# The way back of a Fourier filter, from sums and differences of conjugate pairs in sixteen 32x32 tiles

## The chip, the cores and the metric

The kernel runs on one core of a Trainium2 chip. The metric is the device time of one execution in microseconds; before the change it is 2642.59 us (median of 5 runs, 2641.39 to 2644.59).

## The reference

```python
# x (8, 3008, 256), filt_r and filt_i (1505, 256), w_in (256, 2048), w_out (2048, 256), all fp32
X = np.fft.rfft(x, axis=1)
Y = X * (filt_r + 1j * filt_i)[None]
y = np.fft.irfft(Y, n=3008, axis=1)
h = y.reshape(24064, 256) @ w_in
g = np.where(h > 0, h, np.exp(np.minimum(h, 0)) - 1)
out = g @ w_out
```

Every sequence is filtered along its 3008 positions in the frequency domain, and an ELU layer of two matrix products follows.

## The kernel before, in words

The transform of length 3008 = 47 x 64 is done as matrix products in two steps. Step one (x_unit, a_unit) works on the 64-point part. Step two (b_unit) is the 47-point part: for four frequencies k2 at a time (a group g of eight) it makes real and imaginary parts in PSUM (tiles psr and psi), and multiplies them on DVE with the filter f into four products: sr, si, p and q. On POOL p is added to sr and q to si. The way back starts with bi_unit, 47 points again, from these sums into PSUM (tiles pva and pvb), and ACT copies the result into the tile t3. y_write puts it into DRAM (yd), y_read gets it back in another order, and n_unit does the 64 points of the way back. Between step one and step two the data also goes through DRAM (z_write, z_read).

The ELU layer is done with Strassen-like products of seven terms instead of eight: up_steps makes seven products with w_in (L421, tiles phs, pha, phd), forms sums on DVE (L429, "add b22" and its like), and applies the ELU with ACT (L438, L439) and DVE (L443); down_steps makes the seven products with w_out (L503, PSUM tiles po) and sums them at the last of four (L519, in part deferred as c_unit). o_unit transposes on DVE and writes the output.

All runs in an order written out by hand. A batch has 24 quads; a quad is one pass of the outermost loop, with seven U steps (s1, s2, s6, s5, s7, s3, s4: two matmuls each of 128x128 by 256 columns, or 224 for m = 0) and seven D steps, in the order "UUDUDDU", place 0, "DUUDUDD", place 1. In quads of the set `opens` the order is "DUUDUDDU", place 0, "DUUDUD", place 1. The units of the filter are put into place 0 or place 1 of a quad by a dictionary. So the filter of batch b runs between the matrix products of batch b - 1. Batch 0 is filtered ahead of the loop, in a part of its own (0 to 96 us).

Four PSUM banks (psM, tags m0 to m3) go round between the U steps and the units: `banks` is a list in order of release, a unit takes its first ones and puts them back when they are read.

b_unit and bi_unit do not use the PE array as one 128x128 array. Their inputs lie in partitions 0 to 47 (LO) and 64 to 111 (HI), and their outputs in partitions 0 to 63 and 64 to 127, so that four matmuls work in four separate 64x64 tiles of the array; the rows of a tile are given by the partitions of the input, its columns by the partitions of the output. Per batch there are eight b_units, in quads 9 to 16 of the batch (place 1), and eight bi_units, two quads behind.

The special tables for group 0 (index 1 of gb, gr and gi) hold the frequencies k2 = 0 and 32, which pair with themselves.

Timing of the units in a batch (quads from the batch's start t; a number above 23 lies in the next batch): x_unit 1, 1, 4, 4, 7, 7, each pair with an a_unit in the same quad; f_read and z_read of group g in 7 + g; b_unit in 9 + g; bi_unit and y_write of group g in 11 + g; n_unit in 20, 25, 29, 32, 36, 40; c_unit of half m in 24 + 4 m + 5, o_unit one later. Seen from the following batch, c_unit so stands in quads 5, 9, 13, 17, 21 and 1, and o_unit in 6, 10, 14, 18, 22 and 2.

f_read is issued from POOL's queue; x_load, z_write, z_read, y_write, y_read and the output writes from SP's.

Of the kernel before, what the change touches and what calls it, by code (L numbers as in the profile page):

```python
# [11 lines left out]
FP32 = mybir.dt.float32  # L12
U32 = mybir.dt.uint32
AXT = mybir.ActivationFunctionType
ALU = mybir.AluOpType
# [11 lines left out]
P = 128  # L27
D = 256
# [3 lines left out]
K2 = 32  # L32
XC = 4
NXC = H // XC
NG = K2 // 4
# [6 lines left out]
def _make_tables():  # L42
# [51 lines left out]
    gr[0:24, 1, 0:24], gr[24:48, 1, 24:48] = m0 * c0.T, m3 * c3.T  # L94
    gi[0:24, 1, 24:48], gi[24:48, 1, 0:24] = -m0 * s0.T, -m3 * s3.T
    lie = np.concatenate([2 * np.arange(24), 2 * np.arange(24) + 1])
    gb[:, :, lie] = gb[:, :, :48].copy()
# [6 lines left out]
    once = np.stack([np.eye(P), gf.reshape(P, P)], 1)  # L104
    return [t.astype(np.float32) for t in (ta, tn, np.stack([gb, gr, gi], 1), tf, once)]

# [7 lines left out]
def kernel(  # L114
# [10 lines left out]

    ta_d, tn_d, gs_d, tf_d, once_d = [
        nc.inline_tensor(t, name=n + "_t").ap()
        for t, n in zip(_make_tables(), ("ta", "tn", "gs", "tf", "once"))
    ]

    def pool(name, bufs, **kw):
        return ctx.enter_context(tc.tile_pool(name=name, bufs=bufs, **kw))
# [7 lines left out]
    t2p = pool("t2p", 2)  # L140
    sp = pool("sp", 2)
    qp = pool("qp", 1)
    t3p = pool("t3p", 2)
    t4p = pool("t4p", 2)
# [6 lines left out]

    gs = glob.tile([P, 3, 2, 64], FP32, name="gs")
    gb, gr, gi = (gs[:, i] for i in range(3))

# [3 lines left out]
    edges = glob.tile([P, 2], FP32, name="edges")  # L158
    fd = fdp.tile([NG, 2, 48, 2, 2, D], FP32, name="fd")

    xs, tas, tns, t1s, t2s, ss, t3s, t4s, zs, yds, ys, g_of, po_of, cs_, sds = ({} for _ in range(15))
# [8 lines left out]
    def bank(name, shape=(P, 2, D)):  # L170
        i = banks.pop(0)
        return i, psM.tile(list(shape), FP32, tag="m%d" % i, name=name)
# [120 lines left out]

    def f_read(b, g, t=None):
        t = fbufs[(b * NG + g) % FBUFS] if t is None else t
        for a, r in enumerate((LO, HI)):
            nc.gpsimd.dma_start(t[r].rearrange("p c u d -> p (c u d)"), fd[g, a].rearrange("q c u d -> q (c u d)"))

    def tile_mm(ps, table, k, rhs, special):
# [3 lines left out]

    def b_unit(b, g, f=None, gb=gb, pq=None, between=None):
        t = t2s.pop((b, g))
        f = fbufs[(b * NG + g) % FBUFS] if f is None else f
        (i0, re), (i1, im) = (bank(n) for n in ("psr", "psi"))
        for o, a in ((0, 0), (64, 2)):
            for ps, k in ((re, LO), (im, HI)):
                tile_mm(ps[o:o + 64], gb, k, [t[:, a:a + 2, :]], g == 0 and a == 0)  # L310
        if between:
            between()
        sr, si = (sp.tile([P, 2, D], FP32, tag=n, name=n) for n in ("sr", "si"))
        p, q = pq or (qp.tile([P, 2, D], FP32, tag=n, name=n) for n in ("sp", "sq"))

        nc.vector.tensor_tensor(out=sr, in0=re, in1=f[:, 0], op=ALU.mult)
        nc.vector.tensor_tensor(out=si, in0=re, in1=f[:, 1], op=ALU.mult)
        nc.vector.scalar_tensor_tensor(out=p, in0=im, scalar=-1.0, in1=f[:, 1], op0=ALU.mult, op1=ALU.mult)  # L318
        nc.vector.tensor_tensor(out=q, in0=im, in1=f[:, 0], op=ALU.mult)
        banks.extend((i0, i1))  # L320
        if b == 0:

            ss[b, g] = [sr, p], [si, q]
            return
        nc.gpsimd.tensor_tensor(out=sr, in0=sr, in1=p, op=ALU.add)  # L325
        nc.gpsimd.tensor_tensor(out=si, in0=si, in1=q, op=ALU.add)
        ss[b, g] = [sr], [si]

    def bi_unit(b, g):
        s = ss.pop((b, g))  # L330
        t = t3s[b, g] = t3p.tile([P, 4, D], FP32, tag="t3", name="t3")
        if b == 0:

            pa, pb = (psO.tile([P, 2, 256], FP32, tag="po%d" % i, name="po%d" % i)
                      for i in ((0, 1) if g > 2 and g % 2 else (2, 3)))
        else:
            (i0, pa), (i1, pb) = (bank(n) for n in ("pva", "pvb"))
        for o, table, sv in ((0, gr, s[0]), (64, gi, s[1])):
            for ps, k in ((pa, LO), (pb, HI)):
                tile_mm(ps[o:o + 64], table, k, sv, g == 0 and k == LO)  # L340
        nc.scalar.activation(out=t[:, 0:2, :], in_=pa, func=AXT.Copy)  # L341
        nc.scalar.activation(out=t[:, 2:4, :], in_=pb, func=AXT.Copy)
        if b > 0:
            banks.extend((i0, i1))

    def y_write(b, g, queues=(nc.sync, nc.sync)):
        if g == 0:
            yds[b] = yd.tile([K2, 96, D], FP32, tag="yd", name="yd")
        t = t3s.pop((b, g))
        for a, r in enumerate((LO, HI)):  # L350
            queues[a].dma_start(yds[b][4 * g:4 * g + 4, 48 * a:48 * a + 48, :].rearrange("u r d -> r u d"), t[r])

# [285 lines left out]
    def f_arrange():  # L638

        for c, src in enumerate((filt_r, filt_i)):  # L640
# [14 lines left out]
            nc.gpsimd.dma_start(fd[0, 0, 47:48, c, 1, :], raw(src, 4, [[D, 1], [1, D]]))  # L655

    with tc.manual_schedule():


        with tc.tile_pool(name="boot", bufs=1) as bp:  # L660
            ff = bp.tile([P, NG, 2, 2, D], FP32, name="ff")
            once = bp.tile([P, 2, P], FP32, name="once")
            eye, gf = once[:, 0], once[:, 1].rearrange("p (v q) -> p v q", v=2)
            pq = [bp.tile([P, 2, D], FP32, name="pq%d" % i) for i in range(2)]
            zt[0] += [bp.tile([P, 16 * ROWS], FP32, name="zt%d" % i) for i in range(2)]
# [50 lines left out]
            for g in range(NG):  # L716
                f_read(0, g, ff[:, g])
                if 3 <= g < 5:
                    w_fetch(g + 7)
# [6 lines left out]
            for g in range(NG + 2):  # L726
                back = (lambda g=g: bi_unit(0, g - 2)) if g >= 2 else None
                if g < NG:
                    b_unit(0, g, ff[:, g], gf, pq if g % 2 else None, back)
                else:  # L730
                    back()
                if g < 4:
                    t_first(g + 4)
                if g < 5:
                    w_float(g + 7)
                if g < 3:
                    w_join(g + 7)
                    w_split(g + 8)
                if g == 2:
                    w_split(11)  # L740
                if g >= 2:
                    y_write(0, g - 2, (nc.sync, nc.scalar if g == NG + 1 else nc.sync))
                if g == 7:
                    w_join(10)
                    w_join(11)
                    w_split(12)
                    w_split(13)
# [19 lines left out]
        PER = 24  # L767

        plan, opens = {}, set()

        def at(quad, place, fn, *a):
            plan.setdefault((quad, place), []).append((fn, a))
# [5 lines left out]
        for c in range(2, XBUFS):  # L778
            at(c - 2, 0, x_load, 1, c)
        for i, f in enumerate(fbufs):  # L780
            at(3 + i, 1, nc.vector.memset, f, 0.0)
        for b in range(B):
            t = (b - 1) * PER
            if b > 0:
                for c, s in enumerate((1, 1, 4, 4, 7, 7)):
                    at(t + s, 0, x_unit, b, c)
                    if c % 2 == 0:
                        opens.add(t + s + 1)
                        at(t + s, 1, a_unit, b, c)
                    nb, nxt = (b, c + XBUFS) if c + XBUFS < NXC else (b + 1, c + XBUFS - NXC)  # L790
                    if nb < B:
                        at(t + s, 1, x_load, nb, nxt)
                    at(t + s, 1, z_write, b, c)
                for g in range(NG + 2):
                    s = t + 9 + g
                    if g >= 2:
                        at(s, 1, bi_unit, b, g - 2)
                    if g < NG:
                        at(s, 1, b_unit, b, g)
                    if g >= 2:  # L800
                        at(s, 1, y_write, b, g - 2)
                for g in range(NG):
                    s = t + 7 + g
                    at(s, 1, f_read, b, g)
                    at(s, 1, z_read, b, g)
            for m, (s, place) in enumerate(((20, 0), (25, 1), (29, 1), (32, 0), (36, 0), (40, 0))):
                if b > 0 or m > 0:
                    at(t + s - (1 if m == 0 else 2), 0, tn_read, b, m)
                    at(t + s - (1 if m == 0 else 2), 0, y_read, b, m)
                    at(t + s, place, n_unit, b, m)  # L810
                at(t + PER + 4 * m + 5, 0, c_unit, b, m)
                at(t + PER + 4 * m + 6, 0, o_unit, b, m)
# [54 lines left out]
```

## Time and profile before

| What | Value |
|---|---|
| Median of 5 runs | 2642.59 us |
| Profiled execution | 2641.94 us, span 2640.2 us |
| Granted TensorE clock, mean of the span | 0.991 |
| PE busy | 2588.1 us (98%) |
| DVE busy | 1846.2 us (70%) |
| ACT busy | 1509.1 us (57%) |
| POOL busy | 236.3 us (9%) |
| DMA | 202.85 MB, mean 77 GB/s |
| L503 matmuls (down) | x5376, 1297.9 us busy |
| L302 matmuls to pva and pvb (bi_unit, batches 1 to 7) | x476, mean 564 and 614 ns |
| L302 matmuls to psr and psi (b_unit, batches 1 to 7) | x476, mean 570 ns |
| L325 adds on POOL | x56, mean 1270 ns |

The profile is one execution taken by the hardware profiler. PE is TensorE's matmul, PEld its weight load, which overlaps with matmuls; DVE is VectorE, ACT ScalarE, POOL GpSimd, SP SyncE. L302 is line 302 of the kernel before. An fp32 matmul leaves two records. Their ends are modelled and neighbours overlap, so starts tell more than durations. A line of the timeline has the start in us, the time from the first start to the last end of the merged instructions, engine, line, operation, out<-in, tile shape, operand shape and count; in brackets the idle time ahead of it and what ended it.

### The profile page before, as it was taken

Reading aid. Unit: us, or ns where it says so; the run is one execution under the profiler, and the core shown is the slowest. Engines: PE = TensorE matmul, PEld = TensorE weight load, DVE = VectorE, ACT = ScalarE, POOL = GpSimd, SP = SyncE. Lnnn points to the kernel's source line nnn. Section 1 sums busy time; section 2 is a strip of 40 time slices with the busy share of each in tenths; the row PEclk is TensorE's granted clock in tenths of the full one; section 3 lists DMA queues with packets and bytes.
Section 4 is the critical chain, followed back from the end, with each engine's and each line's share of the span. In section 5 each row is a group of like instructions: output and inputs, shape, how many; then the busy total and the mean of one; then the engine's idle time right before and its main releaser. Section 6 shows DMA issues by size and latency. Waiting matters only on the chain.

```text
span 2640.2 us, 37281 instructions
## 1 busy us (share of the span) xinstructions
PE 2588.1 (98%) x13508; PEld 2216.1 (84%) x13508; DVE 1846.2 (70%) x3203; ACT 1509.1 (57%) x2622; POOL 236.3 (9%) x298
## 2 busy tenths in 40 slices
PE   5899999999999999999999999999999999999998
PEld 4688789887898888988889888898789987898887
DVE  6886766677666776767667776767766767666666
ACT  6665555655555555555555555565555655555554
POOL 5001100012000210002100020001200011000000
PEclk8899999999999999999999999999999999999999
DMA  9534312432124331333204341043321233110010
GB/s 289 149 87 110 84 35 64 107 94 75 46 63 114 83 78 40 75 101 100 75 20 103 88 115 45 21 109 106 98 50 41 71 90 80 39 41 20 22 28 17
DMA packets 224456, 202.85 MB, mean 77 GB/s; under 512 B 127586, under 2 KB 191090, under 8 KB 224272
## 3 DMA queue, kind: packets, MB, share of 16 engines
q1 hardware_dynamic: 211632, 166.70, 24.9%
q0 software_dynamic: 11184, 33.04, 4.8%
q8 instruction: 107, 1.75, 0.3%
q10 hardware_dynamic: 1456, 0.72, 0.1%
q14 instruction: 77, 0.63, 0.1%
HBM read 128.52 MB, written 74.97 MB: 77 GB/s over the span
## 4 chain that ended last, share of the span: by engine, by line
PE 96%; DMA 2%; DVE 1%; ACT 1%; issue 0%; SPq 0%; DVEq 0%; ACTq 0%
PE po L503 43%; PE phs L421 25%; PE phd L421 12%; PE pha L421 6%; PE psn L373 3%; PE pva L302 2%; PE psr L302 2%; PE psa L211 2%; DMA xc<-in_x_dram 1%; DMA x<-in_x_dram 0%; DMA yd<-t 0%; DVE g L429 0%; ACT e L438 0%; PE po L302 0%; PE po L274 0%
## 5 line engine op out<-in xcount | busy, mean ns | idle before, releaser
L503 PE MATMUL po<-g,wo 128*128 128x256 f32 (+1 forms) x5376 | 1297.9, 375 | 0.0
L503 PEld LDWEIGHTS po<-g,wo 128*128 128x128 f32 x5376 | 1016.7, 190 | 121.7 <-issue 5.4
L432 ACT ACTIVATE g<-phs 128x512 f32<-128x512 f32 (+1 forms) x576 | 338.4, 588 | 830.3 <-PE phs L421 830.2
L429 DVE TENSOR_TENSOR g<-phd,g 128x512 f32<-128x512 f32 (+1 forms) x384 | 259.6, 676 | 419.2 <-ACT e L439 355.8
L439 ACT ACTIVATE e<-e 128x512 f32<-128x512 f32 (+1 forms) x768 | 477.1, 621 | 24.3
L421 PE MATMUL phs<-y,wi 128*128 128x256 f32 (+1 forms) x1536 | 395.6, 380 | 0.0
L421 PE MATMUL phs<-ys,wi 128*128 128x256 f32 (+1 forms) x1536 | 387.7, 375 | 1.7 <-ACT g L432 1.5
L443 DVE SCALAR_TENSOR_TENSOR g<-e,g 128x512 f32<-128x512 f32 (+1 forms) x576 | 387.2, 672 | 0.5 <-ACT e L439 0.2
L438 ACT ACTIVATE e<-g 128x512 f32<-128x512 f32 (+1 forms) x576 | 353.0, 613 | 36.0 <-DVE g L429 28.4
L421 PEld LDWEIGHTS phs<-y,wi 128*128 128x128 f32 x1536 | 285.6, 190 | 83.5 <-ACT t L341 34.1
L421 PEld LDWEIGHTS phs<-ys,wi 128*128 128x128 f32 x1536 | 291.3, 190 | 35.8 <-ACT g L432 2.7
L443 DVE SCALAR_TENSOR_TENSOR g<-e,phs 128x512 f32<-128x512 f32 (+1 forms) x192 | 129.8, 676 | 135.9 <-ACT e L439 135.9
L421 PE MATMUL phd<-ys,wi 128*128 128x256 f32 (+1 forms) x768 | 194.5, 376 | 3.3 <-DVE g L429 3.3
L421 PE MATMUL pha<-y,wi 128*128 128x256 f32 (+1 forms) x768 | 193.8, 375 | 0.0
L421 PE MATMUL phd<-y,wi 128*128 128x256 f32 (+1 forms) x768 | 193.7, 375 | 0.0
L438 ACT ACTIVATE e<-phs 128x512 f32<-128x512 f32 (+1 forms) x192 | 112.9, 588 | 140.1 <-PE phs L421 140.0
L325 POOL TENSOR_TENSOR sr<-sr,sp 128x512 f32<-128x512 f32 x56 | 71.1, 1270 | 1158.4 <-DVE sp L318 1158.4
L421 PEld LDWEIGHTS phd<-ys,wi 128*128 128x128 f32 x768 | 145.2, 190 | 22.4 <-DVE g L429 5.9
L421 PEld LDWEIGHTS pha<-y,wi 128*128 128x128 f32 x768 | 146.1, 190 | 16.6
L421 PEld LDWEIGHTS phd<-y,wi 128*128 128x128 f32 x768 | 145.8, 190 | 16.5
L429 DVE TENSOR_TENSOR g<-pha,g 128x512 f32<-128x512 f32 (+1 forms) x192 | 129.1, 673 | 28.7 <-PE pha L421 28.3
L480 DVE TENSOR_TENSOR g<-g,g 128x512 f32<-128x512 f32 (+1 forms) x192 | 130.7, 681 | 6.7
(132 smaller groups left out, 2343.1 us busy)
## 6 DMA issues: line engine op xcount, KB each, us to landing
yd<-t SPq DMA_DIRECT2D x127, 192.0 KB
t<-yd SPq DMA_DIRECT2D x190, 128.0 KB
z<-t SPq DMA_DIRECT2D x84, 256.0 KB
f<-fd POOLq DMA_DIRECT2D x112, 192.0 KB, 3.6
t<-z SPq DMA_DIRECT2D x224, 96.0 KB
out_dram<-o SPq DMA_DIRECT2D x632, 32.0 KB
tn<-tn_t SPq DMA_DIRECT2D x48, 256.0 KB
xc<-in_x_dram SPq DMA_DIRECT2D x84, 128.0 KB
```

What stands on the lines that cost most here:

```text
L211: nc.tensor.matmul(p[o:o + 64, u, :], w[r, u, o:o + 64], src[r, u, :], start=True, stop=True)
L302: nc.tensor.matmul(ps[:, u:u + w, :], table[k, v, :], r[k, u:u + w, :], start=n == 0, stop=n == len(rhs) - 1)
L325: nc.gpsimd.tensor_tensor(out=sr, in0=sr, in1=p, op=ALU.add)
L373: nc.tensor.matmul(ps[:, ts(q, P)], t[:, i - 4 * m, ds(dh * P, P)], w[:, i - 4 * m, :], start=True, stop=True)
L421: nc.tensor.matmul(ps[:, a, 0:h], w_in[q][:, COMBO[n], a, :], y[n], start=start and a == 0, stop=True, skip_group_check=True)
L429: nc.vector.tensor_tensor(out=g[o], in0=i0, in1=i1, op=ALU.add)
L432: nc.scalar.activation(out=g[o], in_=i0, func=AXT.Copy)
L438: nc.scalar.activation(out=e, in_=src, func=AXT.Relu, scale=-1.0)
L439: nc.scalar.activation(out=e, in_=e, func=AXT.Exp, scale=-1.0)
L443: nc.vector.scalar_tensor_tensor(out=g[n], in0=es[n], scalar=1.0, in1=src, op0=ALU.subtract, op1=ALU.max)
L480: nc.vector.tensor_tensor(out=b12, in0=b22, in1=b12, op=ALU.subtract)
L503: nc.tensor.matmul(po[i][:, u, 0:h], w_out[q][:, COMBO[n], a, :], g[n][:, a, :], start=q == 0 and a == 0 and n in (1, 3, 6, 4), stop=True, ...
```

## The change

For batches 1 to 7, b_unit's table is cut into two times 32 columns (24 used): the 47 output rows of a frequency now come as two sets of 24, a frequency and its conjugate partner, in the same partitions and in two halves of the free dimension. Each of the four k2 of a group has a 32-column tile of its own. So there are 16 matmuls of 256 columns in eight 64x32 tiles. The products on DVE stay. POOL adds p to sr and q to si as before, and then forms the sum and the difference of the two halves of each (four more instructions of 256 columns; for group 0 three copies put the self-paired frequencies back). The result z of two groups lies in one tile. bi_unit runs once for two groups: 16 matmuls of 24 rows by 32 columns (24 used) and 512 columns, one in each of the sixteen 32x32 tiles, into four PSUM banks, then four copies on ACT. y_write writes two groups with four DMAs.

The filter is arranged for this layout once more in DRAM (fp, by f_pairs, 14 DMAs from POOL's queue in quads 1 to 4), and f_read takes four DMAs of 24 rows instead of two of 48.

The plan changes with it: b_units in quads 9, 10, 12, 13, 15, 16, 18, 19, bi_units and y_writes in 11, 14, 17, 20; x_units in 2, 2, 4, 4, 7, 7; n_unit of m = 0 in 23 instead of 20, of m = 5 in 41 instead of 40; the quads behind a bi_unit join `opens`. Batch 0 keeps the old code as b_first, bi_first and y_write_first, with its buffers put elsewhere.

```diff
-    sp = pool("sp", 2)
+    sp = pool("sp", 1)
     qp = pool("qp", 1)
-    t3p = pool("t3p", 2)
+    t3p = pool("t3p", 1)
...
+    def f_read(b, g):
+        t = fbufs[(b * NG + g) % FBUFS]
+        for a in range(4):
+            nc.gpsimd.dma_start(t[32 * a:32 * a + 24].rearrange("p c u d -> p (c u d)"),
+                                fp[g, a].rearrange("q c u d -> q (c u d)"))
...
+    def b_unit(b, g):
+        t = t2s.pop((b, g))
+        f = fbufs[(b * NG + g) % FBUFS]
+        (i0, re), (i1, im) = (bank(n) for n in ("psr", "psi"))
+        for c in range(2):
+            for a in range(4):
+                for ps, k in ((re, LO), (im, HI)):
+                    nc.tensor.matmul(ps[32 * a:32 * a + 32, c, :], fb[k, 1 if g == a == 0 else 0, c, :], t[k, a, :],
+                                     start=True, stop=True)
+        sr, si = (sp.tile([P, 2, D], FP32, tag=n, name=n) for n in ("sr", "si"))
+        if g % 2 == 0:
+            ss[b, g] = qp.tile([P, 4, 2, D], FP32, tag="z", name="zs")
+        z = ss[b, g - g % 2][:, :, g % 2]
+        p, q = z[:, 0:2], z[:, 2:4]
+        products(re, im, f, sr, si, p, q)
+        banks.extend((i0, i1))
+        nc.gpsimd.tensor_tensor(out=sr, in0=sr, in1=p, op=ALU.add)
+        nc.gpsimd.tensor_tensor(out=p[:, 0], in0=sr[:, 0], in1=sr[:, 1], op=ALU.add)
+        nc.gpsimd.tensor_tensor(out=p[:, 1], in0=sr[:, 0], in1=sr[:, 1], op=ALU.subtract)
+        nc.gpsimd.tensor_tensor(out=si, in0=si, in1=q, op=ALU.add)
+        nc.gpsimd.tensor_tensor(out=q[:, 0], in0=si[:, 0], in1=si[:, 1], op=ALU.subtract)
+        nc.gpsimd.tensor_tensor(out=q[:, 1], in0=si[:, 0], in1=si[:, 1], op=ALU.add)
+        if g == 0:
+            nc.gpsimd.tensor_copy(out=p[0:32], in_=sr[0:32])
+            for i in range(2):
+                nc.gpsimd.tensor_copy(out=q[0:32, i], in_=si[0:32, 1 - i])
+
+    def bi_unit(b, g):
+        z = ss.pop((b, g))
+        t = t3s[b, g] = t3p.tile([P, 2, 4, D], FP32, tag="t3", name="t3")
+        pv = [bank("pv") for _ in range(4)]
+        for p in range(4):
+            for a, (_, ps) in enumerate(pv):
+                for js, v in ((slice(0, 1), 1), (slice(1, 2), 0)) if g == a == 0 else ((slice(0, 2), 0),):
+                    r = slice(32 * a, 32 * a + 24)
+                    nc.tensor.matmul(ps[32 * p:32 * p + 32, js, :], bb[r, v, p, :], z[r, p, js, :],
+                                     start=True, stop=True, tile_position=(32 * a, 32 * p))
+        for a, (i, ps) in enumerate(pv):
+            nc.scalar.activation(out=t[:, :, a, :], in_=ps, func=AXT.Copy)
+            banks.append(i)
...
+        t = t3s.pop((b, g)).rearrange("p j a d -> p (j a) d")
+        for p in range(4):
+            nc.sync.dma_start(yds[b][4 * g:4 * g + 8, 24 * p:24 * p + 24, :].rearrange("u r d -> r u d"),
+                              t[32 * p:32 * p + 24])
...
+    def f_pairs(c, u):
+        src = fd.rearrange("g a q c u d -> (g a) q c u d")[:, :, c, u, :]
+        dst = fp.rearrange("g (a u) k c h d -> (g a) u k c h d", u=2)[:, u, :, c, :, :]
+        nc.gpsimd.dma_start(dst[:, :, 0, :], src[:, 0:48:2, :])
+        nc.gpsimd.dma_start(dst[:, 1:24, 1, :], src[:, 1:46:2, :])
+        nc.gpsimd.dma_start(dst[:, 0, 1, :], src[:, 47, :])
+        if u == 0:
+            nc.gpsimd.dma_start(dst[0, :, 1, :], src[0, 1:48:2, :])
...
-                for c, s in enumerate((1, 1, 4, 4, 7, 7)):
+                for c, s in enumerate((2, 2, 4, 4, 7, 7)):
...
-                for g in range(NG + 2):
-                    s = t + 9 + g
-                    if g >= 2:
-                        at(s, 1, bi_unit, b, g - 2)
-                    if g < NG:
-                        at(s, 1, b_unit, b, g)
-                    if g >= 2:
-                        at(s, 1, y_write, b, g - 2)
                 for g in range(NG):
-                    s = t + 7 + g
-                    at(s, 1, f_read, b, g)
-                    at(s, 1, z_read, b, g)
-            for m, (s, place) in enumerate(((20, 0), (25, 1), (29, 1), (32, 0), (36, 0), (40, 0))):
+                    s = t + 9 + g + g // 2
+                    at(s, 1, b_unit, b, g)
+                    at(s - 2, 1, f_read, b, g)
+                    at(s - 2, 1, z_read, b, g)
+                    if g % 2:
+                        opens.add(s + 2)
+                        at(s + 1, 1, bi_unit, b, g - 1)
+                        at(s + 1, 1, y_write, b, g - 1)
+            for m, (s, place) in enumerate(((23, 0), (25, 1), (29, 1), (32, 0), (36, 0), (41, 0))):
```

## The prediction

> **What bounds the kernel now.** I read the page first: the shares of the engines, then the chain that ended last.
>
> ```profile
> PE 2588.1 (98%) x13508; PEld 2216.1 (84%) x13508; DVE 1846.2 (70%) x3203; ACT 1509.1 (57%) x2622; POOL 236.3 (9%) x298
> ...
> PE 96%; DMA 2%; DVE 1%; ACT 1%; issue 0%; SPq 0%; DVEq 0%; ACTq 0%
> PE po L503 43%; PE phs L421 25%; PE phd L421 12%; PE pha L421 6%; PE psn L373 3%; PE pva L302 2%; PE psr L302 2%; PE psa L211 2%; DMA xc<-in_x_dram 1%; DMA x<-in_x_dram 0%; DMA yd<-t 0%; DVE g L429 0%; ACT e L438 0%; PE po L302 0%; PE po L274 0%
> ```
>
> PE carries 96% of the chain: what a change does to PE's stream is what it does to the time. The lines the change touches (pva and psr at L302) are 4%, some 105 us, so no more than that is at stake in gain. The busy figures overlap, since records of matmuls run into each other, so I count from start to start in the timeline of PE. Ahead of it: an fp32 matmul leaves two records, and one record of 256 columns steps by 0.216 us (eight of L503 from 236.25 end at 237.98). The first excerpt is a quad whose end holds b_unit alone, the second one with bi_unit and b_unit.
>
> ```profile
> 236.25 1.89 PE L503 MATMUL po<-g,wo 128*128 128x256 f32 x8
> 238.07 0.64 PE L302 MATMUL psr<-t,gs 48*64 48x512 f32 x1
> ...
> 238.57 0.59 PE L302 MATMUL psi<-t,gs 48*64 48x512 f32 x1
> 239.09 1.13 PE L421 MATMUL phs<-y,wi 128*128 128x256 f32 x4
> 240.06 1.03 PE L421 MATMUL pha<-y,wi 128*128 128x256 f32 x4
> ```
> ```profile
> 280.33 1.24 PE L503 MATMUL po<-g,wo 128*128 128x256 f32 x5
> 281.50 0.64 PE L302 MATMUL pva<-sr,gs 48*64 48x512 f32 x1
> ...
> 281.52 0.64 PE L302 MATMUL pvb<-si,gs 48*64 48x512 f32 x1
> ...
> 282.86 0.59 PE L302 MATMUL psi<-t,gs 48*64 48x512 f32 x1
> 283.38 1.13 PE L421 MATMUL phs<-y,wi 128*128 128x256 f32 x4
> 284.34 1.03 PE L421 MATMUL pha<-y,wi 128*128 128x256 f32 x4
> ```
>
> Four matmuls in the four 64x64 tiles start 7 ns apart and run together. I call that a round, and a stay in tiles, from the last full matmul's end to the next one's start, a visit. Alone: 239.09 - 237.98 = 1.11 us, and the four records after it take 0.97 (240.06 - 239.09) where four steps are 0.86: 0.11 more, so 1.22. Two rounds: 280.33 + 5 x 0.216 = 281.41, 283.38 - 281.41 = 1.97, plus 0.96 - 0.86 = 0.10, so 2.07. A round is the difference, 0.86 us (512 columns, two records of 0.43), and a visit costs 0.36 beside its rounds.
>
> **The change part by part.** All counts are for each of seven batches (1 to 7); batch 0 keeps its own code.
>
> Rounds removed. Before: b_unit 8 rounds, bi_unit 8 rounds. Visits: quads 9 and 10 hold b_unit alone, 11 to 16 both, 17 and 18 bi_unit alone: 10 visits with 16 rounds, 6 x 2.07 + 4 x 1.22 = 17.3 us. After: b_unit issues 16 matmuls of 256 columns into eight 64x32 tiles, twice each, as many columns per tile as before, one round; bi_unit issues 16 of 512 columns into sixteen 32x32 tiles, one round for two groups, so 4. No quad holds both: 12 visits with one round each, 12 x 1.22 = 14.6. Gain 2.7 a batch, 19 us in seven. The four visits' worth of rounds saved would be 3.4; the two extra visits take 0.7 of it.
>
> More tiles start later. The starts above are 7 ns apart. Eight tiles have 4 starts more than the measured visit, sixteen 12 more: 8 x 0.028 + 4 x 0.084 = 0.56 a batch, 4 us in seven. Between 0 (the starts hide behind the first record) and 13 ns a start (the widest step, 238.07 to 238.08 is 10), 7 us.
>
> That the tiles do stream together is the step everything hangs on. The trace has two column tiles beside two row tiles, never four. Below, a round stays 0.86; above, only two column tiles run at once and each round costs 0.86 more. I take the lower end: two rounds in four tiles add exactly what their columns take, nothing is lost to sharing so far. Nor has PE issued a visit's 64 records in 0.86 us (a_unit's 64, half of them loads, take 1.89), but four loads and four matmuls are out within 21 ns of the first start.
>
> The Trainium skill, "TensorE: Matmul & The Clock Gate", section "Measured speedup vs the span model", gives 10.6 times for sixteen tiles, not 16. Read as a rate, a bi_unit round would last 16/10.6 of 0.86, 1.30 us, and as an estimate from that page 28 rounds lose 12 us and the gain is all but gone. The same table explains its own figure by the span of one burst, whose fixed part is in my 0.36; no run here shows sixteen tiles yet.
>
> POOL work. It has two adds of 512 columns per group; four of 256 come on top.
>
> ```profile
> 286.47 1.26 POOL L325 TENSOR_TENSOR sr<-sr,sp 128x512 f32<-128x512 f32 x1 [9.51 <-DVE sp L318]
> 287.70 1.26 POOL L326 TENSOR_TENSOR si<-si,sq 128x512 f32<-128x512 f32 x1
> 288.92 1.04 POOL L297 DMA_DIRECT2D f<-fd  x2
> ```
>
> Half of 1.26 each makes 2.5 + 4 x 0.63 = 5.0 us, so POOL would end at 291.5 in this quad; bi_unit comes at the quad's end, here 295.7 (the next start of L302), less 0.86. Margin 3 us, cost 0. For group 0 three copies add some 2.5, with a further quad of room. The four reads of the filter take 4 x 0.52 us instead of 2 x 0.52 on POOL's queue, behind the adds and two quads ahead of their use: 0. f_pairs issues 14 DMAs in quads 1 to 4, 7 to 11 us of a POOL that is idle there, and moves some 3 MB; first use in quad 7, 40 us on: 0. If that cover were gone, quad 9's products would wait, once.
>
> DVE beside a longer POOL. This is the cover that is thin. Quad 13 of a batch, where c_unit stands in place 0:
>
> ```profile
> 331.74 1.27 POOL L325 TENSOR_TENSOR sr<-sr,sp 128x512 f32<-128x512 f32 x1 [14.44 <-DVE sp L318]
> 332.77 0.53 DVE L519 TENSOR_TENSOR k<-k,c 128x256 f32<-128x256 f32 x1
> 332.97 1.45 POOL L326 TENSOR_TENSOR si<-si,sq 128x512 f32<-128x512 f32 x1
> 333.33 1.37 DVE L519 TENSOR_TENSOR c<-c,k 128x256 f32<-128x256 f32 x1
> 334.62 0.41 DVE L519 TENSOR_TENSOR c<-po,k 128x256 f32<-128x256 f32 x1
> ```
>
> An add with both operands in SBUF takes 0.42 without POOL (L519's median) and 1.37 against it; one with an operand in PSUM keeps 0.41. Behind c_unit stands add b22 (L429), and PE's step s4 waits for that. Three of c_unit's four adds are exposed, to a POOL that now works until 5 us after its start. Before, c_unit ended at 335.37 and phd, from 334.66 four steps long, at 335.5: spare 0.15, and add b22 may come 1 us late before s4 (1.73 us after s7, less its own 0.69) stands. After, the quad ahead holds no bi_unit, so PE is 0.86 sooner; quad 12 opens with a D step, so its DVE tail ends 0.86 later (quad 16 doesn't, but quad 17 has n_unit's combine too); one more blocked add costs up to 0.63. 0.86 + 0.86 + 0.63 - 0.15 - 1.0 = 1.2 at worst, 0 at best, in quads 13 and 17. I take 0.15 in each, 2 us in all; the worst is 2 x 7 x 1.2 = 17.
>
> Banks. bi_unit takes all four and the next quad opens with a D step. a_unit already does so in a quad of the same order, and its visits show no wait beyond the fixed part: 0, at most one ACT copy of 0.60 for each of 28, 17 us.
>
> Moves. The first x_units go from quad 1 (with c_unit) to quad 2 (with o_unit). In quad 1 PE waits on DVE:
>
> ```profile
> 436.25 0.62 DVE L429 TENSOR_TENSOR g<-phd,g 128x448 f32<-128x448 f32 x1
> 436.92 1.02 PE L421 MATMUL phd<-ys,wi 128*128 128x224 f32 x4 [0.52 <-DVE g L429]
> ```
>
> c_unit is 4 x 0.42 = 1.7, o_unit two transposes, 1.3: the wait may shrink to 0 or double. Between -4 and +4 us over the batches; I take 0. n_unit of half m = 0 gets three more quads, its reads two; y_write, z_read and y_read keep their order on SP. Where y_write waits for ACT, z_read and the output writes are queued behind it, as now; same bytes. Batch 0: t3 becomes halves of one tile. 0 as they are disjoint; if a half waited for the other's write (3.71 us, DMA yd<-t in the chain), up to 6 x 3.7 = 22 us.
>
> Sum: -19 + 4 + 2 = -13. The profiled execution took 2641.94 (span 2640.20); the median of five is 0.65 above: 2641.94 - 13 + 0.65 = 2629.6, said as 2629.5.
>
> **The rivals.**
> A, slower: the place is the visits of b_unit and bi_unit, the mechanism that only two of the four column tiles stream at a time. Every round costs 0.86 more: 12 x 0.86 x 7 = 72, 2702. Half of the loss is 2665. It decides as soon as a round is above 1.02 us (0.86 + 13/84). For it: the trace never has four. Against: starts 7 ns apart, no loss with two. 0.12.
> B, about the same: the thin DVE cover is gone at its worst (17 instead of 2) or the banks are (17): 2644 to 2647. For it: 1.37 against 0.42; against: 2.73 us of DVE idling ahead of add b22 in quads without c_unit. 0.15, of which a tail beyond the band.
> C, more gain: starts hidden and the quad 1 wait gone: -19 - 4 = -23, 2620. 0.10; it adjoins the forecast.
> D: the halves of batch 0 serialise or another wait: 2640 to 2652. 0.05.
>
> **How the numbers follow.** My forecast has 0.58. Its own range is 2619 to 2638. For 8 in 10 it must reach into B: 2617 to 2648; outside lie A and small tails. About 0.2% (5 us) is what a measurement of this kernel can tell from no change: faster by that is the forecast, C and a little of B, 0.70; the same, B and D for the most part, 0.14; slower, A and the tails, 0.16.
>
> **What would show it.** PE's timeline: sixteen matmuls of bb starting within 0.1 to 0.2 us in one visit of 1.2 to 1.3 us, as b_unit's; 12 visits a batch. A visit near 2.1 means rival A. POOL's busy time some 150 to 250 us higher. In quads 13 and 17, phd<-ys (s4) with an idle time released by DVE L429 means B; idle before bb released by ACT or DVE means banks. The span from 0 to 96 us should not move.

## The result and the profile after

The changed kernel takes 2636.42 us (median of 24 runs, 2633.34 to 2639.18), the kernel before 2642.25 (44 runs over several chips). The ratio is 0.9978, with a 95% interval of 0.9972 to 0.9983: 5.8 us faster. The forecast was 13 us and 2629.5. The sign is right and the time lies in the range, but 7 us of the forecast gain did not come.

The profiled execution took 2638.83 us (span 2636.8). From the page, the engines and the chain by engine:

```profile
PE 2579.3 (98%) x15300; PEld 2217.9 (84%) x15300; DVE 1862.2 (71%) x3203; ACT 1504.8 (57%) x2622; POOL 489.3 (19%) x669
...
PE 95%; DVE 1%; ACT 1%; DMA 0%; issue 0%; DVEq 0%; SPq 0%; ACTq 0%
```

PE still carries the chain. POOL's busy time is 253 us higher, just above what was forecast (150 to 250). So I count PE from start to start again, and from here on a visit goes from the start of the last full record to the start of the next one. That is 0.216 more than the prediction's figure: its 1.11 is 1.33 here.

In the timeline of PE, a b_unit (eight tiles) in quad 16, and a bi_unit (sixteen tiles) of groups 2 and 3 in quad 14:

```profile
321.74 1.03 PE L571 MATMUL po<-g,wo 128*128 128x256 f32 x4
322.69 0.40 PE L376 MATMUL psr<-t,pairs 48*32 48x256 f32 x1
...
323.72 1.13 PE L489 MATMUL phs<-y,wi 128*128 128x256 f32 x4
```
```profile
294.19 1.89 PE L571 MATMUL po<-g,wo 128*128 128x256 f32 x8
296.01 1.14 PE L407 MATMUL pv<-zs,pairs 24*32 24x512 f32 x32
297.08 1.13 PE L571 MATMUL po<-g,wo 128*128 128x256 f32 x4
```

The first is 321.74 + 3 x 0.216 = 322.39 to 323.72, 1.33 us, as long as a visit of b_unit alone before. The second is 294.19 + 7 x 0.216 = 295.70 to 297.08, 1.38 us: twelve more starts than in four tiles cost 0.05. Sixteen tiles stream together. The bi_unit of groups 0 and 1, in quad 11, is another matter:

```profile
251.18 1.89 PE L571 MATMUL po<-g,wo 128*128 128x256 f32 x8
253.00 2.14 PE L407 MATMUL pv<-zs,pairs 24*32 24x256 f32 x40
255.07 1.13 PE L571 MATMUL po<-g,wo 128*128 128x256 f32 x4
```

252.69 to 255.07, 2.38 us: a whole 0.99 us more than its sisters, in every batch, for a work of the same number of columns in each tile. Its count is 40 records and not 32, since in the row of tiles of k2 = 0 each half of the columns has a table of its own.

Quad 17, where n_unit of m = 5 stands behind c_unit, on DVE, on POOL and on PE:

```profile
332.36 1.05 DVE L464 TENSOR_TENSOR ys<-y 128x256 f32<-128x256 f32 x1 [0.36 <-ACT y L443]
333.52 0.76 DVE L465 TENSOR_TENSOR y<-y,y 128x256 f32<-128x256 f32 x1
334.20 0.94 DVE L466 TENSOR_TENSOR ys<-y,ys 128x256 f32<-128x256 f32 x1
335.18 0.42 DVE L467 TENSOR_TENSOR ys<-y,ys 128x256 f32<-128x256 f32 x1
335.53 0.68 DVE L497 TENSOR_TENSOR g<-phd,g 128x512 f32<-128x512 f32 x1
```
```profile
331.68 1.45 POOL L388 TENSOR_TENSOR si<-si,zs 128x512 f32<-128x512 f32 x1
333.21 0.79 POOL L389 TENSOR_TENSOR zs<-si 128x256 f32<-128x256 f32 x1
333.96 0.91 POOL L390 TENSOR_TENSOR zs<-si 128x256 f32<-128x256 f32 x1
```
```profile
336.26 1.13 PE L489 MATMUL phd<-ys,wi 128*128 128x256 f32 x4 [0.99 <-DVE g L497]
```

n_unit's combine is four operations with all operands in SBUF. While POOL works they take 1.05, 0.76 and 0.94 us; the fourth, after POOL's end at 334.87, takes 0.42. Add b22 (L497) comes late, and s4 on PE waits 0.99 us.

The excerpts of DVE and POOL fit together closely: each of the three slowed operations ends 0.28 us after the POOL instruction during which it started (333.41 after 333.13, 334.28 after 334.00, 335.14 after 334.87). So it is in quads 13 and 17 of every batch, before and after, for each DVE add or subtraction of 256 columns with both operands in SBUF that starts during a POOL add (0.277 to 0.287 us). c_unit's add with an operand in PSUM, which starts during POOL's add too, takes its 0.41.

The view of waits tells what PE waited for in the whole execution, as a sum, a number of times and the longest, here of before and of after:

```profile
PE phd L421 <- DVE g L429: 3.3, 7, 0.5
```
```profile
PE phd L489 <- DVE g L497: 7.0, 7, 1.0
```

The numbers look like the same wait doubled. They are two: before, six stand in quad 1 (0.52 each) and one of 0.16 in quad 3 of the first batch; after, all seven stand in quad 17. Quad 1 of the batch shown in the prediction now starts s4 without any wait:

```profile
437.94 0.92 PE L489 MATMUL phd<-ys,wi 128*128 128x224 f32 x4
```

I summed PE's start-to-start intervals from the first product with w_in to the last matmul. Steps beyond 0.216 in visits, behind visits (about 0.104 each) and elsewhere are kept apart; elsewhere they are called stalls. Steps that are only a few ns off are in none of the rows, so the rows' differences leave 0.5 us over.

| us | before | after |
|---|---|---|
| total | 2530.8 | 2525.6 |
| visits of b_unit and bi_unit (70, then 84) | 114.1 | 102.1 |
| records behind all visits | 9.5 | 10.9 |
| a_unit and n_unit | 125.6 | 125.4 |
| stalls | 8.7 | 13.8 |

So the tiles gave 12.0 - 1.4 = 10.5 us, and stalls took 5.1 back.

### The profile page after: what moved, and what is told of

Its sections match the earlier page's. It is cut to its first block, busy times and chain, and to the rows that moved or that the text cites. A ratio compares the mean times of both kernels' runs of the same rounds, so it can differ in the third digit from the quotient of the medians.

```text
span 2636.8 us, 41233 instructions
## 1 busy us (share of the span) xinstructions
PE 2579.3 (98%) x15300; PEld 2217.9 (84%) x15300; DVE 1862.2 (71%) x3203; ACT 1504.8 (57%) x2622; POOL 489.3 (19%) x669
## 4 chain that ended last, share of the span: by engine, by line
PE 95%; DVE 1%; ACT 1%; DMA 0%; issue 0%; DVEq 0%; SPq 0%; ACTq 0%
PE po L571 43%; PE phs L489 25%; PE phd L489 12%; PE pha L489 6%; PE psn L441 3%; PE psr L376 2%; PE psa L228 2%; PE pv L407 1%; DVE ys L464 0%; PE po L324 0%; DMA yd<-t 0%; DVE ys L466 0%; PE psi L376 0%; ACT e L507 0%; DVE g L497 0%
## 5 line engine op out<-in xcount | busy, mean ns | idle before, releaser
L497 DVE TENSOR_TENSOR g<-phd,g 128x512 f32<-128x512 f32 (+1 forms) x384 | 259.5, 676 | 402.9 <-ACT e L507 345.6
L511 DVE SCALAR_TENSOR_TENSOR g<-e,g 128x512 f32<-128x512 f32 (+1 forms) x576 | 397.2, 690 | 1.6 <-ACT e L507 1.3
L385 POOL TENSOR_TENSOR sr<-sr,zs 128x512 f32<-128x512 f32 x56 | 71.3, 1272 | 1144.4 <-DVE zs L330 1144.4
L497 DVE TENSOR_TENSOR g<-pha,g 128x512 f32<-128x512 f32 (+1 forms) x192 | 129.2, 673 | 53.3 <-PE pha L489 53.1
```

Source lines behind the costliest of these rows:

```text
L497: nc.vector.tensor_tensor(out=g[o], in0=i0, in1=i1, op=ALU.add)
L511: nc.vector.scalar_tensor_tensor(out=g[n], in0=es[n], scalar=1.0, in1=src, op0=ALU.subtract, op1=ALU.max)
```

## The experiments

The theory: two things eat the gain, bi_unit of group 0 by the order in which its matmuls are issued (W in the expectations), and n_unit in quad 17 by POOL's four sums and differences; and the move of the x_units gives something. The rivals: that group 0 pays for twenty matmuls instead of sixteen in whatever order; that c_unit ahead of n_unit, and not POOL, makes quad 17 late; that the move of the x_units gives nothing, as forecast. All are compared with runs of the kernel before on the same chip.

**The changed kernel again**, as the measure for the others.

> The changed kernel once more, beside the kernel before on the same chip. Both theories of its loss (a late last part of bi_unit's visit for group 0, DVE held up in quad 17) expect the same as measured: 2636 us, 0.2% under before; visits of bi_unit 1.38 us from the last full matmul's start to the next one's, for group 0 2.37; a wait of PE on DVE of about 1.2 us in quad 17 and 0.15 in quad 13 of every batch.

2636.75 us against 2641.61, ratio 0.9981 (0.9973 to 0.9990). The count of PE's starts gives 2525.59, as in the first profile (2525.61).

**The order in bi_unit of group 0.** The plain order puts a second half (256 columns) right behind the first half in the same tile, four times among the sixteen. Here the four second halves come last.

```diff
-        for p in range(4):
-            for a, (_, ps) in enumerate(pv):
-                for js, v in ((slice(0, 1), 1), (slice(1, 2), 0)) if g == a == 0 else ((slice(0, 2), 0),):
...
+        work = [(p, a, slice(0, 1) if g == a == 0 else slice(0, 2), 1 if g == a == 0 else 0)
+                for p in range(4) for a in range(4)]
+        if g == 0:
+            work += [(p, 0, slice(1, 2), 0) for p in range(4)]
+        for p, a, js, v in work:
```

> Group 0's second halves (four matmuls of 256 columns into the row of tiles that already has a first half) are issued after all sixteen first ones, not between them. Theory W (PE holds some 16 matmuls at a time; the four that wait for a busy tile take places in it, and the last three wait until those leave): the visit of group 0 falls from 2.37 to 1.38-1.40 us, 7 x 0.98 = 6.9 us less in all, 2629.5. Rival R (twenty matmuls, or two for one tile, cost this much in any order): it stays at 2.37 and the time at 2636.4.

2633.10 us, ratio 0.9964 (0.9951 to 0.9976): 3.6 better than the changed kernel on the same chip, half of what was expected. PE's timeline, and the weight loads (PEld) of the same visit:

```profile
246.44 1.89 PE L573 MATMUL po<-g,wo 128*128 128x256 f32 x8
248.26 1.71 PE L409 MATMUL pv<-zs,pairs 24*32 24x256 f32 x40
249.90 1.13 PE L573 MATMUL po<-g,wo 128*128 128x256 f32 x4
```
```profile
248.25 0.78 PEld L409 LDWEIGHTS pv<-zs,pairs 24*32 24x32 f32 x36 [0.33 <-issue]
249.34 0.15 PEld L409 LDWEIGHTS pv<-zs,pairs 24*32 24x32 f32 x4 [0.30 <-issue]
```

The visit falls from 2.38 to 1.95 us (247.95 to 249.90). The order matters, but it doesn't reach 1.38. The loads tell why (two for each fp32 matmul): 33 are out within 0.25 us of the first and the 34th at 0.46, those of 17 matmuls; the two of the 18th come 0.65 and 0.68 us after the start, when the first, of 256 columns, has ended; the last four come at 249.34, 1.08 us after the start, when the second and third, of 512 columns, have ended. That refines the theory: some 17 matmuls can be under way, and they leave in the order of the program, whichever tile they use. With the changed kernel's order the three matmuls behind the seventeenth are of 512 columns, so a second round begins: they start 0.86, 1.08 and 1.10 us after the first one there, though no other matmul of the visit uses their tiles. With this order three short ones are late behind long ones.

**Short ones first.** By the refined theory the four first halves (256 columns) must be the first to leave, so that the last three can enter early. This kernel has, beside that, n_unit's move of the next experiment; its base is the kernel with both.

```diff
         if g == 0:
+            work.sort(key=lambda w: w[1] > 0)
             work += [(p, 0, slice(1, 2), 0) for p in range(4)]
```

> The version with both edits, in which group 0's four first halves (256 columns) are issued ahead of the twelve matmuls of 512 columns, then the four second halves. Theory W2 (17 matmuls are in flight at most, and they leave in program order, each when it has ended): the 18th to 20th wait only for short ones, 0.6 us after the first start instead of 1.06, and the visit falls from 1.95 to 1.50 us, 7 x 0.45 = 3.2 us less than with both edits. Rival R2 (a second matmul for a tile costs what it does wherever it stands): 1.95 as before, no gain.

2621.70 us against 2641.67, ratio 0.9925 (0.9912 to 0.9937), 3.1 better than its base on the same chip. The visit:

```profile
248.86 1.89 PE L574 MATMUL po<-g,wo 128*128 128x256 f32 x8
...
251.90 1.13 PE L574 MATMUL po<-g,wo 128*128 128x256 f32 x4
```

250.37 to 251.90, 1.53 us; the last six weight loads come 0.65 to 0.71 us after the first. The same twenty matmuls took 2.38, 1.95 and 1.53 us in three orders: order alone makes 0.85 of the loss of 0.99. Whether the 0.15 left over 1.38 is the price of twenty matmuls instead of sixteen was not tested. What it is that has some 17 places these runs do not tell. The Trainium skill, "TensorE: Matmul & The Clock Gate", "Architectural detail: the array is 16× 32×32, not 1× 128×128", gives PE a queue 64 deep that can pull weight loads ahead; whether the 68 records of 17 matmuls are that queue, no run here shows.

**n_unit of m = 5 out of quad 17.** It goes to quad 18, where no c_unit stands ahead of it.

```diff
-            for m, (s, place) in enumerate(((23, 0), (25, 1), (29, 1), (32, 0), (36, 0), (41, 0))):
+            for m, (s, place) in enumerate(((23, 0), (25, 1), (29, 1), (32, 0), (36, 0), (42, 0))):
```

> n_unit of m = 5 moves from quad 17 (41) to quad 18 (42), in which POOL has no adds. If PE's wait in quad 17 comes from n_unit's four subtractions standing behind c_unit while POOL works, it falls from 1.16 us to about the 0.15 of quad 13, and quad 18 shows none (quad 12, built alike, has none): 7 x 1.0 = 7 us less, 2629.4. If it comes from c_unit and the longer POOL alone, the wait in quad 17 stays above 0.8 and the time at 2636.

2626.31 us, ratio 0.9939 (0.9927 to 0.9952), 10.4 better than the changed kernel on the same chip. The wait of phd (s4) for add b22 is in none of its quads, and the count of stalls falls from 13.8 to 4.6.

**Quad 17 without POOL's sums.** The move takes n_unit away from POOL and from c_unit at once. This kernel leaves n_unit where it is and omits POOL's four sums and differences of group 5 alone, the group whose b_unit stands in quad 16; that part of the output is not formed.

```diff
-        nc.gpsimd.tensor_tensor(out=p[:, 0], in0=sr[:, 0], in1=sr[:, 1], op=ALU.add)
...
+        if g != 5:
+            nc.gpsimd.tensor_tensor(out=p[:, 0], in0=sr[:, 0], in1=sr[:, 1], op=ALU.add)
...
```

> The changed kernel without POOL's four sums and differences for group 5 alone (its way back is then made from the products of p and q, so the result of these frequencies is left out); POOL's two adds of 512 columns stay. Group 5's adds are the ones that run in quad 17. Theory P (n_unit's four subtractions, both operands in SBUF, are blocked by POOL's longer work): they fall from 1.05, 0.76, 0.94 and 0.42 us to 0.42 each, PE's wait in quad 17 from 1.16 us to under 0.2, 7 us less than the changed kernel, 2629.5. Rival O (the order alone, n_unit behind c_unit in one quad, one b_unit ahead): the wait stays above 0.9, the time at 2636.5.

2625.68 us, ratio 0.9938 (0.9920 to 0.9956), stalls 4.5 (two runs): by the count of starts 9.3 us, where the move of n_unit gave 9.2. DVE's timeline in quad 17:

```profile
327.49 0.43 DVE L466 TENSOR_TENSOR ys<-y 128x256 f32<-128x256 f32 x1
328.02 0.43 DVE L467 TENSOR_TENSOR y<-y,y 128x256 f32<-128x256 f32 x1
328.36 0.42 DVE L468 TENSOR_TENSOR ys<-y,ys 128x256 f32<-128x256 f32 x1
328.81 0.42 DVE L469 TENSOR_TENSOR ys<-y,ys 128x256 f32<-128x256 f32 x1
```

1.7 us where it was 3.2. With the sums gone the combine is short again and nothing waits, with c_unit still ahead of it: the four instructions on POOL are the cause.

**Both mends**, the order with second halves last and n_unit in quad 18, on two chips.

> Both edits. They touch different visits, so their gains should add: 2636.4 - 6.9 - 7 = 2622.5, 0.75% under before. If a wait hides behind the one removed (banks, the next place), less than that: above 2626.

> The version with both edits again, on the same chip as the one with the short ones first: 2624.8 as before; the one with the short ones first is 3.2 us under it by theory W2, equal by R2.

2624.80 us, ratio 0.9935 (0.9922 to 0.9949), and 2624.84, ratio 0.9934 (0.9920 to 0.9947). On the first chip that is 11.9 better than the changed kernel, less than the 3.6 + 10.4 of the medians alone. By the count of starts the parts are 3.5 and 9.2 alone, 11.9 together. Most of the 0.8 between lies in the first quad of the loop, whose small waits make 1.6 to 2.1 us in these profiles; the visits of group 0 give 3.0 and quad 17 gives 8.8 both alone and together.

**The x_units alone.** The kernel before with nothing but their move to quad 2, together with what the plan ties to them: the a_unit, x_load and z_write beside them, and the quad behind that joins `opens`.

```diff
-                for c, s in enumerate((1, 1, 4, 4, 7, 7)):
+                for c, s in enumerate((2, 2, 4, 4, 7, 7)):
```

> The kernel before with one thing of the change alone: the first two x_units, and the a_unit behind them, in quad 2 instead of 1. If the wait of 0.65 us in quad 1 of six batches came from c_unit and the x_units standing together, it goes: 6 x 0.65 = 3.9 us less, 2637.9. If it only moves to quad 2, where o_unit and the end of n_unit's subtractions are, a wait of 0.4 to 0.9 us shows there and the time stays at 2641.8.

2636.42 us against 2641.67, ratio 0.9976 (0.9967 to 0.9986): 5.2 us, as much as the whole change. Stalls fall from 8.7 to 2.8, and PE's wait for add b22 is no longer in the view of waits.

**The change without that move**, the other way round: x_units back in quads 1, 1, 4, 4, 7, 7.

> The changed kernel with the first two x_units and their a_unit back in quad 1, as before the change. Theory S (the move's gain of some 5.5 us and the rest of the change add up): 2636.5 + 5.5 = 2642, no difference from the kernel before that can be measured, with a wait of 0.65 us in quad 1 of six batches. Rival M (the move helps only the old schedule; the new one, with b_units three quads longer and n_unit elsewhere, takes the wait up anyway): the time stays at 2636.5 to 2638.

2642.84 us against 2642.24, ratio 0.9999 (0.9990 to 1.0008): with the x_units left where they were, the tiles, the sums and the new quads together are worth nothing that can be measured. That the change is faster at all is due to the move. The view of waits has now both stalls, fourteen instead of seven:

```profile
PE phd L489 <- DVE g L497: 10.2, 14, 1.0
```

The best version, with short halves first and n_unit in quad 18, is faster than both kernels: 20 us below before.

## Why the prediction was right and wrong, step by step

**Rounds: right.** The forecast was 17.3 us of visits a batch before and 14.6 after, with 0.56 more for starts. By the counts (visits and 0.104 behind each) it was (114.1 + 70 x 0.104) / 7 = 17.3 before and (102.1 + 84 x 0.104) / 7 = 15.8 after. Without the 0.99 of group 0 the latter is 14.8.

**Rival A: out.** The visits of b_unit and bi_unit are 1.33 and 1.38 us, 1.12 and 1.16 in the prediction's measure. The rate read out of the skill's 10.6 ("TensorE: Matmul & The Clock Gate", "Measured speedup vs the span model") would have needed 0.44 more. That table's own explanation, the span of one burst, is the one that agrees.

**Starts: mis-sized.** 0.028 and 0.084 us were taken for a visit of eight and of sixteen tiles, 4 us in all. 0.005 and 0.052 were measured, 1.7 us. The starts hide in part, as the lower bound had it.

**bi_unit of group 0: a step that failed.** "16 of 512 columns into sixteen 32x32 tiles, one round for two groups, so 4" holds for three visits of four. I read the loop's special case for g == a == 0 as the same columns in each tile, which it is, and not as twenty matmuls in an order that puts one in wait four times. 7 x 0.99 = 7 us. The trace of before did not show it: there, too, group 0 has two halves in a row in one tile, but no visit has more than ten matmuls, and the visits of group 0 take 1.34 and 2.20 us where the others take 1.33 and 2.19.

**DVE beside a longer POOL: mis-sized, and the term that decided.** Place and mechanism were named: quads 13 and 17, operands in SBUF against POOL, add b22, s4. (The excerpt headed "Quad 13", from 331.74, is quad 17; quad 13 has the same 0.53 and 1.37 from 274.33.) From 0 to 1.2 us a quad I took 0.15 in each, 2 us in all. In quad 13 s4 came 0.155 us late and the start behind it 0.104 more, 0.26 in all (1.8 us). In quad 17 it was 1.16 and 0.10, 1.26 in all, above the worst of 1.2: 8.8 us (9.2 by the difference of the counts). "Quad 17 has n_unit's combine too" stood in the text, but the price was made from c_unit's adds and one blocked add; the combine's own four operations, all with operands in SBUF, were not put against POOL's four new ones. c_unit itself fares a little better than before: its blocked adds take 0.83 and 0.61 instead of 1.37 and 0.41. And POOL's 256 columns were taken as half of 1.26: they take 0.73 in the median, 0.79 and 0.91 in quad 17 beside DVE, and up to 1.26 elsewhere. The Trainium skill, "SBUF — State Buffer", "SBUF: two separate sides", calls the port pair of DVE and GpSimd an exclusive lock, by which the later one waits for a whole instruction; 1.05, 0.76 and 0.94 instead of 0.42, each ending 0.28 us after POOL's instruction, agree.

**Moves: a term taken at 0 that made the sign.** The wait in quad 1 was shown, and a range of -4 to +4 us was given because o_unit might take c_unit's place as a hindrance. I took 0. Quad 2 has no wait at all: the move is worth 5.2 us by the medians, 6.0 by the count (2530.8 - 2524.8), nearly all in stalls, and more than the range allowed. In quad 1 s4 came 0.68 us late in six batches and the start behind it 0.10 more, 6 x 0.79 = 4.7 us; quad 3 of the first batch gave 0.7 more, in all 5.4. The move takes x_units, a_unit and an `opens` quad along, and which of them counts was not tried apart.

**Banks, f_read, f_pairs, y_write and the halves of batch 0: right at 0.** No wait before bi_unit's matmuls is released by ACT or DVE, and rival D is in none of the views.

The sum by the measured terms, in us of PE's starts: -17.5 for rounds and starts, +7 for group 0's visits, +10.6 for DVE in quads 13 and 17, -5.4 for the moves, 0.1 left over: -5.2. Against the forecast (-19 + 4, 0, +2 and 0) that is -2.5, +7, +8.6 and -5.4. So two steps failed at a cost of 15.6 us, and two misses on the good side gave 7.9 of it back. That the sign is right is luck: it comes from the move, which the forecast took at 0, and without it the change gains nothing (2642.84 against 2642.24). A time inside the range says little for the sum behind it.

## What to carry to other kernels

Where many small matmuls share the array, the order of issue is part of the price: put those that end early first. Here four pairs in a row into one tile cost 0.99 us a visit, and the best of three orders 0.15. Before new work goes to POOL, list every DVE operation whose operands are all in SBUF in the stretch that POOL now fills, each as ending about 0.28 us after the POOL instruction that it meets (0.42 became 0.76 to 1.05 here), and not only the ones that a trace already shows blocked. A change that carries several moves is worth undoing one by one: here one changed line of the plan carried the whole measured gain.

## Not expected of the hardware

The limit of some 17 fp32 matmuls under way, leaving in program order across separate tiles, is read from the weight loads above and foretold the third order (1.50 us expected, 1.53 measured). It is the order in which places come free: a matmul for another tile can start ahead of one that waits for its tile, as the nine of 512 columns do that start within 0.10 us in the changed kernel's visit of group 0.

The part ahead of the loop is not as steady as "should not move" had it. Its instructions are the same in all kernels here, though the changed ones place the buffers elsewhere; but the first n_unit starts at 96.4 us in the profile of before, at 99.0 in that of after, and between 94.6 and 99.8 in the others. In the profile of after PE idles 3.3 us there, waiting for DVE at 72.9 us, and b_first's matmuls then take up to 1.11 us where they take 0.64 before the gap; the granted clock is 1.00 before it and 0.50 from 74 to 80 us. Such an idle time does not need the change: it is 2.8 us in the profile of the kernel before with the x_units moved, 1.3 in those of the kernel before and of the changed kernel with the second halves last, and the clock is 0.50 in the profile of before too, from 62 to 70 us. The changed kernel's runs spread over 2633.3 to 2639.2 and the kernel before's over 2638.7 to 2645.5, which is of that size; whether it comes from there is open.
